# Denominators as extra columns of the numerator matmuls, in a linear-attention and mixture-of-experts kernel

## The chip, the core and the metric

The kernel runs on one core of one Trainium2 chip. Its metric is the device time of one execution in microseconds (us). The engines are PE (matmuls, with PEld for its weight loads), DVE (elementwise work), ACT (activations and copies), POOL and SP (which here mostly issue transfers).

## The reference

```python
# per batch b and head h: seq 576, head_dim 64 (8 batches, 8 heads)
q_p, k_p = phi(q), phi(k)                  # phi(x) = x + 1 for x > 0, exp(x) otherwise
kv  = einsum('bhsd,bhse->bhde', k_p, v)
z   = sum(k_p, axis=2)
num = einsum('bhsd,bhde->bhse', q_p, kv)
den = einsum('bhsd,bhd->bhs', q_p, z)[..., None] + 1e-06
x   = (num / den), as 4608 rows of 512
P   = exp(x @ w_gate - max), then 8 times: P /= P.sum(1) + 1e-9; P /= P.sum(0) + 1e-9; P *= N / E
out = sum over 8 experts e of P[:, e] * (relu(x @ w1[e]) @ w2[e])
```

## The kernel before

**Stages.** The front computes the attention in 16 blocks, one for each batch and half of its heads (four heads), and with it expert 0 of the second part on the token groups that are complete. After it come the routing probabilities P (a Sinkhorn loop of eight rounds) beside the rest of expert 0, and from about 172 us experts 1 to 7, in nine units of 512 tokens each, with a seven-product scheme in place of eight block products in both layers (`block7` for the first, `unit` for the second).

**Order.** Nothing is scheduled by hand. Each step is a task of a small planner (`_Plan`), with an engine or a choice of engines, an assumed duration, dependencies, and the buffers it takes and uses; `ranks`, a long string of numbers, gives priorities (and in places the engine) to the tasks of the front. The planner runs through the tasks and emits each step's instructions at its turn, so its order is the program order on each engine. An engine works through its own instructions in that order. The semaphore waits between engines are put in by the layer below, which follows, tile by tile, who reads and writes what; it knows nothing of the planner's buffers.

**One attention block.** k, q and v are loaded (L274, tiles kqin and vin). ACT takes exp (L290), DVE makes `min(max(x + 1, 1), exp x)` into `t` (L303, L306), and v is copied to `vv` beside a column of ones (L234 on ACT, L236 on DVE; these two lines are also all other copies). PE multiplies k^T by v in 18 matmuls (L335) into `kv_ps`, two PSUM banks; the ones give z, the sum of k, as column 65 of each head. That product is masked and moved to `kvz` (L346 on ACT, L348 on DVE). PE transposes q in two pieces of five and four (L363, `qt_ps`) and they are copied to `qpT`. The division then goes like this:

- `f_den` (L378): ten matmuls with the z columns as the moving operand, two columns each, into `den_ps`;
- `f_rd` (L384, L386): DVE adds 1e-6 to the 20 denominators of a row and takes their reciprocals (`rden`);
- `f_num` (L402): ten matmuls of 128 columns into `num_ps`, in three pieces of 4, 4 and 2, each in a PSUM bank of its own;
- `f_xn` (L407): DVE multiplies each piece by the reciprocals into `xn`;
- `f_xt` (L418): PE transposes `xn` in two groups of five, and ACT or DVE copies each (L234, L236) into `xT`.

**PSUM.** Besides the kv pair there is the pool `aps` with two buffers of one bank under the tag "att". In the front `qt_ps`, `den_ps`, `num_ps`, `xt_ps` and the routing logits (`lg_ps`, L437, read by ACT at L441) take turns in it, each as a new tile; later the column sums of the Sinkhorn loop (`cs_ps`, L476), the product R of each pair of `block7` (PE writes at L737 and L742, ACT reads at L771, DVE at L780 as `h<-att`), and one tile of the last unit. The planner's own counterpart is `p_att`, a pool of two. In the first block two of the numerator pieces are in the banks `ye0` and `ye1`.

**Expert work.** `hq` (L590) is the first layer of expert 0, four matmuls of 512 columns to a task, and `ye` (L859) its second; PE fills the front with them. `yw` (L510) are warm-up matmuls on zeros in the first 20 us.

Of the kernel before, what the change touches and what calls it, by code (L numbers as in the profile page):

```python
# [122 lines left out]
def kernel(  # L123
# [35 lines left out]
    aps = ctx.enter_context(tc.tile_pool(name="aps", bufs=2, space=PSUM))  # L159
# [33 lines left out]
    p_vv, p_kvz, p_qpT, p_xn, p_rden = (S_.pool(2) for _ in range(5))  # L193
    p_att, p_hq, p_h = S_.pool(2), S_.pool(2), S_.pool(2)
    p_xst, p_s2, p_s5 = (S_.pool(2) for _ in range(3))
# [48 lines left out]
    v_land, kv_id = [], []  # L244
# [6 lines left out]
    def att(b, g):  # L251
        n = 2 * b + g
        pr = n - 100.0

        def ps_home(i):
            if n < 1 and i < 2:
                return p_ye[i], yps, f"ye{i}"
            return p_att, aps, "att"
# [80 lines left out]
        tkv = fadd(("pe", 0.54), f_kv, deps=[tph["k"]] + tvv, acq=[gkv], use=[gvv, gt["k"]], prio=pr)  # L339
# [17 lines left out]
        for j0, j1 in ((0, 5), (5, NJ)):  # L357
            gp = S_.grp(p_att)

            def f_qt(_, j0=j0, j1=j1, gp=gp):  # L360
                gp["tile"] = aps.tile([P, 5, 2, PW], FP16, tag="att", name="qt_ps")
                for j in range(j0, j1):
                    nc.tensor.transpose(gp["tile"][:, j - j0, :, :].rearrange("p h w -> p (h w)"),  # L363
                                        gt["q"]["tile"][:, j, 2:4, :].rearrange("p r d -> p (r d)"), ident)
# [7 lines left out]
        gden, grd, gxn = S_.grp(p_att), S_.grp(p_rden), S_.grp(p_xn)  # L372

        def f_den(_):
            gden["tile"] = aps.tile([P, 5, 2, 2], FP32, tag="att", name="den_ps")
            for i, j in enumerate(js):
                for hh in range(2):
                    nc.tensor.matmul(gden["tile"][:, i, :, hh],  # L378
                                     lhsT=gq["tile"][:, hh, j:j + 2, :].rearrange("p j w -> p (j w)"),
                                     rhs=gz["tile"][:, hh, :, D], start=True, stop=True)  # L380

        def f_rd(_):
            grd["tile"] = fp.tile([P, 5, 4], FP32, tag="rden", name="rden")
            nc.vector.tensor_scalar(out=grd["tile"], in0=gden["tile"].rearrange("p i r h -> p i (r h)"),  # L384
                                    scalar1=1e-6, scalar2=None, op0=ALU.add)
            nc.vector.reciprocal(grd["tile"], grd["tile"])  # L386
        tden = fadd(("pe", 0.26), f_den, deps=tq + tz, acq=[gden], use=[gq, gz], prio=pr)
        trd = fadd(("dve", 0.5), f_rd, deps=[tden], acq=[grd], use=[gden], prio=pr)

        def f_xa(_):  # L390
            gxn["tile"] = fp.tile([P, 5, 4, D], FP16, tag="xn", name="xn")
        txa = fadd(("none", 0.0), f_xa, deps=[tden], acq=[gxn], prio=pr)
        txn = []
        for i0, i1 in ((0, 2), (2, 4), (4, 5)):
            hn = ps_home(i0 // 2)
            gn = S_.grp(hn[0])

            def f_num(_, i0=i0, i1=i1, gn=gn, hn=hn):
                gn["tile"] = hn[1].tile([P, 2, 2, 2, D], FP32, tag=hn[2], name="num_ps")
                for i in range(i0, i1):  # L400
                    for hh in range(2):
                        nc.tensor.matmul(gn["tile"][:, i - i0, :, hh, :],  # L402
                                         lhsT=gq["tile"][:, hh, js[i]:js[i] + 2, :].rearrange("p j w -> p (j w)"),
                                         rhs=gz["tile"][:, hh, :, 0:D], start=True, stop=True)

            def f_xn(_, i0=i0, i1=i1, gn=gn):
                nc.vector.tensor_tensor(  # L407
                    out=gxn["tile"][:, i0:i1], in0=gn["tile"][:, 0:i1 - i0].rearrange("p i r h e -> p i (r h) e"),
                    in1=grd["tile"][:, i0:i1, :, None].broadcast_to([P, i1 - i0, 4, D]), op=ALU.mult)
            t1 = fadd(("pe", 0.12 * (i1 - i0)), f_num, deps=[tden, txa], acq=[gn], use=[gq, gz], prio=pr)  # L410
            txn.append(fadd(("dve", 0.14 + 0.275 * (i1 - i0)), f_xn, deps=[t1, trd, txa], use=[gn, grd, gxn], prio=pr))
        for c2 in range(2):
            gx = S_.grp(p_att)

            def f_xt(_, c2=c2, gx=gx):
                gx["tile"] = aps.tile([P, S], FP16, tag="att", name="xt_ps")
                for i in range(5):
                    nc.tensor.transpose(gx["tile"][:, 64 * js[i]:64 * js[i] + P],  # L418
                                        gxn["tile"][:, i, 2 * c2:2 * c2 + 2, :].rearrange("p r e -> p (r e)"), ident)
# [10 lines left out]
    def logits(b2):  # L430
        gl = S_.grp(p_att)

        def f_l(_):
            gl["tile"] = aps.tile([P, NJ, E], FP32, tag="att", name="lg_ps")
# [12 lines left out]
    def sinkhorn():  # L447
# [10 lines left out]
        for it in range(8):  # L458
# [15 lines left out]
            def f_c(_, gc=gc):  # L474
                gc["tile"] = aps.tile([P, E], FP32, tag="att", name="cs_ps")
# [20 lines left out]
    gate = const.tile([P, 4], FP32, tag="gate", name="gate")  # L496
    warm = const.tile([P, 512], FP16, tag="warm", name="warm")
# [175 lines left out]
    def block7(e, g, gW, tW):  # L673
# [49 lines left out]
        def pair(gi):  # L723
            gX, gR, gZ, gs2, gs5 = (S_.grp(p) for p in (p_hq, p_att, p_ye[3], *((p_e2, p_e5) if e == 0 else (p_s2, p_s5))))
            kx = {id(gX): (hqp, "hq"), id(gR): (aps, "att")}
# [3 lines left out]
            def pm(lhs, b, w, g_, first, deps, pr):  # L729
                def f_m(_):  # L730
                    if first:
                        pl, tag = kx[id(g_)]
                        g_["tile"] = pl.tile([P, 2, 256], FP32, tag=tag, name=tag)
# [89 lines left out]
    def unit_plain(e, g, gW=None, tW=None):  # L823
# [5 lines left out]
        if e > 0:  # L829
            zp[1], zp[2], zp[3] = (p_ye[0], yps, "ye0"), (p_hq, hqp, "hq"), (p_att, aps, "att")  # L830
# [22 lines left out]
        for tt in range(1 if e > 0 else 0, 4):  # L853
            for half in range(2):
                def f_y(_, half=half, tt=tt):
                    if half == 0:
                        gy[tt]["tile"] = zp[tt][1].tile([P, 512], FP32, tag=zp[tt][2], name=zp[tt][2])
# [237 lines left out]
    for d, k_ in zip(chain, chain[1:]):  # L1095
# [3 lines left out]
        0:-50.0024 36:8.7509 38:8.7566 40:-50.0207 42:-49.9982 43:8.7608 44:-50.0228 45:8.7578 46:-50.0192 47:-50.0138  # L1099
        49:8.7452:act 50:-49.9982 51:-50.0108 52:-50.0204:act 54:8.7572 55:-50.0216 56:8.7563 57:-49.9985:act  # L1100
        58:-50.0222 59:-50.0213 61:-50.0117 62:-50.0036 63:-50.012 64:8.759 65:-50.0135 66:-98.0291 67:-50.012
        68:8.7602:dve 69:-49.9994 70:-50.0129:act 71:-50.015 73:-50.0144 75:-49.9886 77:-50.0129 78:-49.9988
        79:-50.0186 80:8.7587 81:-50.0207 82:-50.0027 84:-50.0198 85:-49.9829 86:-49.9985:act 88:-98.021
        89:-50.015:act 90:-50.0201 91:8.7617:dve 92:-50.0195 93:-50.0219 95:-50.0162 96:8.7575 97:-50.0201 98:-50.0186
        99:8.7464 100:-98.0051 101:-50.0195 102:-50.0144:act 103:-50.0141 104:-50.0198 106:8.7632 108:8.7575
        110:-49.9844 112:-50.0216 114:-50.0006 116:8.7575 117:-50.0132 118:-50.0006 119:-50.021 120:-50.0192
        121:-49.9982 123:-50.0201:dve 124:-50.0159 125:-50.0225:dve 127:-50.0138 128:-50.0105:dve 129:8.762
        130:-50.0213 131:-98.0054 132:-50.0189 134:-49.9787 135:-50.0207 136:-49.9859 137:-50.003 138:-50.0018
        139:-50.0228 140:-50.0153 141:-50.0093:dve 142:-49.9811 143:-50.0003:dve 144:-50.0156 146:-50.012 148:-50.0147
        150:-50.0237 151:-50.021 152:8.7593 153:-50.0204 154:-50.0192 155:-50.0156 157:-50.0003:act 158:-50.0159  # L1110
        159:8.7368:dve 161:-50.0117 162:-50.0147:act 163:-50.0021 164:-50.0213 165:-50.0222 166:8.7443 168:-50.021
        169:-50.0231 170:-50.0168 171:-50.0267 172:-50.0216 173:-50.0144 174:-50.0228 175:-50.0228:dve 176:-50.0201
        177:-49.9787:act 179:-50.0063 181:-50.006 183:-50.0144 184:-50.0189 185:-50.0189 187:-50.0168 189:-50.0048
        191:8.7584 192:-49.9802 193:-50.0225 194:-50.0255 195:-50.0201 196:-50.0219 198:-50.0195 199:-50.0132
        200:-50.0207:dve 202:-50.0249 203:-50.0144 204:-50.0015 205:-50.0213:dve 206:-98.0237 207:-50.012 209:-50.0183
        210:-50.0204 211:-50.0258 212:-50.0288 213:-50.0189 214:-50.0237 215:-49.9808 216:-49.9856:act 217:-50.0219
        218:-50.0117:dve 219:8.7602 221:-50.0153 223:-49.9991 225:-50.0015 226:-50.0165 227:-50.0225 228:-50.0162
        229:-98.0078 230:-50.0165 232:-50.0087:dve 233:-98.0054 234:8.7512:dve 236:-50.0216 237:-98.0051:act
        238:-50.0246 239:-50.0165:dve 240:-50.0219 241:-98.0048 243:-50.027 244:-50.0195 245:-50.0135 246:-50.0126
        247:-50.0228 248:-50.0123 249:-50.0159 250:-50.018:act 251:-98.0228 252:-49.9826 253:-50.018 255:-50.0213  # L1120
        257:-50.018 259:-50.0162 260:-50.0231 261:-98.0063 262:-50.0282 263:-50.012 264:-50.0003 266:-50.0117:dve
        267:-50.0159 268:8.7464:act 270:-50.0195 271:8.7509:act 272:-98.0054 273:-50.0168 274:-50.0162 275:-98.0246
# [125 lines left out]
```

## Time and profile before

| | |
|---|---|
| median of 3 runs (960.19 to 960.27) | 960.21 us |
| the profiled execution, and its span | 960.04 us, 958.3 us |
| PE, DVE, ACT busy | 950.7, 768.7, 571.7 us |
| `den_ps` matmuls in all (L378) | 160, median 166 ns |
| `num_ps` matmuls in all (L402) | 160, median 220 ns |
| DVE for one block's division: L384, L386, L407 | 0.173, 0.278, 2 x 0.684 and 0.419 us |

The profile gives each instruction's start and length on its engine, what ended the idle time before it, and a chain of waits followed back from the last instruction. PE's matmuls are pipelined: a matmul of 512 columns is shown with 379 ns, and the next starts 216 ns after it. What a matmul takes from PE is the step to the next start.

### The profile page before, as it was taken

The numbers are of one execution on the slowest core, as the hardware profiler recorded it, in microseconds if no ns is written. First come the engines' busy times: TensorE is split into PE (matmuls) and PEld (weight loads), VectorE is DVE, ScalarE is ACT, GpSimd is POOL, SyncE is SP. The second block draws the span as 40 slices with busy tenths as digits, with TensorE's granted clock in tenths as the row PEclk, the third lists the DMA queues.
The fourth block names the chain that finished last, engine by engine and source line by source line (L and its number), as shares of the span: only waits on it lengthen the run. The fifth ranks groups of instructions, "written<-read, shape, count | busy, mean of one in ns | idle before, by whom it ended". The sixth has DMA issues, their size and how long they took to land.

```text
span 958.3 us, 18782 instructions
## 1 busy us (share of the span) xinstructions
PE 950.7 (99%) x7265; PEld 650.3 (68%) x7265; DVE 768.7 (80%) x1529; ACT 571.7 (60%) x1032; POOL 153.4 (16%) x199
## 2 busy tenths in 40 slices
PE   9999999999999999999999999999999999999998
PEld 4656666566676667766676666766677666766676
DVE  6988888878887787888877788877878788877776
ACT  6897855765555555555555555555555555555552
POOL 4100000111112211221112211221112211111111
PEclk9999999999999999999999999999999999999999
DMA  9985983344145421544125431644215441425545
GB/s 316 346 313 207 289 261 101 44 100 100 55 133 116 106 81 49 126 110 100 56 89 111 108 94 46 150 103 109 64 61 112 110 99 56 138 78 153 155 106 133
DMA packets 109946, 121.83 MB, mean 127 GB/s; under 512 B 7840, under 2 KB 92960, under 8 KB 109856
## 3 DMA queue, kind: packets, MB, share of 16 engines
q1 hardware_dynamic: 84320, 96.23, 32.1%
q0 software_dynamic: 25136, 23.87, 14.6%
q8 instruction: 57, 0.93, 0.4%
q10 hardware_dynamic: 400, 0.52, 0.2%
q14 instruction: 33, 0.27, 0.1%
HBM read 119.69 MB, written 17.69 MB: 143 GB/s over the span
## 4 chain that ended last, share of the span: by engine, by line
PE 95%; DMA 2%; ACT 1%; DVE 1%; issue 0%; POOL 0%; SPq 0%; DVEq 0%; ACTq 0%
PE ye L997 34%; PE hq L737 20%; PE att L737 10%; PE ye L859 7%; PE Zye L997 6%; PE Zye L737 5%; PE hq L742 4%; PE hq L590 2%; DMA kqin<-in_k_dram 2%; PE att L742 2%; PE Zye L742 1%; PE xt_ps L418 1%; PE kv_ps L335 1%; PE num_ps L402 1%; PE qt_ps L363 1%; ACT e L290 1%
## 5 line engine op out<-in xcount | busy, mean ns | idle before, releaser
L1011 DVE SCALAR_TENSOR_TENSOR acc<-ye,P_sb,acc 128x256 f32<-128x256 f32 x620 | 266.4, 476 | 105.8 <-PE ye L997 104.0
L997 PEld LDWEIGHTS <-S 128*128 128x128 f16 x1984 | 194.1, 98 | 45.9 <-issue 0.2
L1021 POOL TENSOR_TENSOR acc<-acc,h 128x256 f32<-128x256 f32 x124 | 102.9, 847 | 601.1 <-ACT h L1018 601.1
L997 PE MATMUL ye<-h,S 128*128 128x256 f16 x1488 | 192.8, 273 | 0.0
L997 PEld LDWEIGHTS <-h 128*128 128x128 f16 x1488 | 145.6, 98 | 39.9
L777 ACT ACTIVATE h<-hq 128x512 f16<-128x512 f32 x134 | 80.1, 597 | 142.0 <-PE hq L737 124.0
L737 PEld LDWEIGHTS <-W 128*128 128x128 f16 x896 | 87.7, 98 | 81.1
L737 PE MATMUL att<-xs,W 128*128 128x512 f16 x448 | 133.2, 379 | 0.0
L737 PE MATMUL hq<-xs,W 128*128 128x512 f16 x448 | 133.2, 379 | 0.0
L737 PE MATMUL hq<-xs,w 128*128 128x512 f16 x448 | 124.1, 379 | 0.0
L780 DVE CUSTOM_DVE_ANT_0 h<-att,s 128x512 f16<-128x512 f32 x126 | 86.4, 686 | 23.5 <-ACT s L764 23.0
L737 PEld LDWEIGHTS <-w 128*128 128x128 f16 x672 | 65.8, 98 | 54.5
L774 ACT ACTIVATE h<-Zye 128x512 f16<-128x512 f32 x134 | 80.1, 598 | 35.2 <-PE Zye L737 28.0
L1018 ACT ACTIVATE h<-Zye,P_sb 128x256 f32<-128x256 f32 x124 | 52.1, 471 | 78.1 <-PE Zye L997 78.1
L764 ACT COPY s<-hq 128x512 f32<-128x512 f32 x126 | 73.5, 583 | 35.4 <-PE hq L737 31.3
L780 DVE CUSTOM_DVE_ANT_0 h<-hq,s 128x512 f16<-128x512 f32 x126 | 86.3, 685 | 9.0 <-PE hq L737 9.0
L757 ACT COPY Zye<-hq 128x512 f32<-128x512 f32 x134 | 77.9, 581 | 20.2 <-PE hq L737 17.0
L968 DVE TENSOR_TENSOR S<-h 128x1024 f16<-128x1024 f16 x124 | 84.7, 683 | 5.8 <-ACT h L777 5.8
L771 ACT COPY s<-att 128x512 f32<-128x512 f32 x126 | 74.5, 591 | 0.0
L859 PE MATMUL ye<-w,h 128*128 128x512 f16 x296 | 73.8, 379 | 0.0
L737 PE MATMUL Zye<-xs,w 128*128 128x512 f16 x224 | 66.6, 379 | 0.0
L997 PE MATMUL Zye<-w,h 128*128 128x256 f16 x496 | 64.3, 273 | 0.0
(119 smaller groups left out, 1096.1 us busy)
## 6 DMA issues: line engine op xcount, KB each, us to landing
xs<-xd SPq DMA_DIRECT2D x196, 256.0 KB, 4.1
w<-in_moe_w_dram POOLq DMA_DIRECT2D x48, 256.0 KB, 4.2
out_dram<-acc SPq DMA_DIRECT2D x67, 128.0 KB, 2.4
kqin<-in_k_dram SPq DMA_DIRECT2D x12, 576.0 KB, 5.6
kqin<-in_q_dram SPq DMA_DIRECT2D x12, 576.0 KB, 6.8
vin<-in_v_dram SPq DMA_DIRECT2D x12, 576.0 KB, 7.7
xs<-xd SPq DMA_DIRECT2D x49, 128.0 KB, 2.5
xd<-xT SPq DMA_DIRECT2D x27, 128.0 KB, 6.2
```

The lines of the kernel that those rows point to most:

```text
L737: nc.tensor.matmul(dst, lhsT=lhs(0, c), rhs=X(b)(c), start=(first and c == 0), stop=(c == 1), skip_group_check=True)
L757: nc.scalar.copy(out=Zt[1], in_=gX["tile"])
L764: nc.scalar.copy(out=gs2["tile"], in_=gX["tile"])
L771: nc.scalar.copy(out=gs5["tile"], in_=gR["tile"])
L774: nc.scalar.activation(out=hd(0, 0), in_=Zt[1], func=AF.Relu)
L777: nc.scalar.activation(out=hd(1, 0), in_=gX["tile"], func=AF.Relu)
L780: nc.vector._custom_dve(TENSOR_ADD_SAT, out=dst, in0=ps, in1=sb, s0=3.0e38, s1=0.0)
L859: nc.tensor.matmul(gy[tt]["tile"], lhsT=hx(f, P * tt, P), rhs=gw2["tile"][:, f, :], start=(f == 0), stop=(f == NFT - 1))
L968: nc.vector.tensor_tensor(out=gS[i]["tile"], in0=a0, in1=a1, op=op)
L997: nc.tensor.matmul(bank(g_)[:, s, :], lhsT=lhs(s, kk), rhs=rhs(kk), start=(new and s == 0 and kk == 0), stop=(kk == 3), skip_group_check=True)
L1011: nc.vector.scalar_tensor_tensor(out=dst(), in0=bank(g_)[:, s, :], scalar=P_sb[:, gg, e:e + 1], in1=dst(), op0=ALU.mult, op1=ALU.add)
L1021: nc.gpsimd.tensor_tensor(out=dst(), in0=dst(), in1=gst["tile"], op=ALU.add)
```

## The change

The separate denominator matmuls go. Each numerator matmul takes all of a head's 65 columns of `kvz` for both row halves, 130 columns, so that every 65th output column is a denominator. The ten matmuls are in two pieces: six into the two kv banks and four into both att banks. For each piece the denominators get their 1e-6 (`f_ra`, on ACT or DVE as the planner chooses), DVE takes reciprocals and multiplies. `att2` is now one tile of both att banks, allocated once; `att_bank` gives the half whose turn it is, to every user of the old tag. Two dependencies are new: a block's kv product waits for piece A of the block two before, and piece A for that of the block before. The string `ranks` is new throughout, and with it the order of the front.

```diff
-    aps = ctx.enter_context(tc.tile_pool(name="aps", bufs=2, space=PSUM))
+    aps = ctx.enter_context(tc.tile_pool(name="aps", bufs=1, space=PSUM))
...
+    att2 = aps.tile([P, 2, 512], FP32, tag="att", name="att")
+
+    def att_bank(dt=FP32):
+        b = att2[:, (len(p_att["order"]) - 1) % 2]
+        return b if dt == FP32 else b.bitcast(dt)
...
-        tkv = fadd(("pe", 0.54), f_kv, deps=[tph["k"]] + tvv, acq=[gkv], use=[gvv, gt["k"]], prio=pr)
+        tkv = fadd(("pe", 0.54), f_kv, deps=[tph["k"], num_a[n - 2] if n > 1 else None] + tvv, acq=[gkv],
+                   use=[gvv, gt["k"]], prio=pr)
...
-                gp["tile"] = aps.tile([P, 5, 2, PW], FP16, tag="att", name="qt_ps")
+                gp["tile"] = att_bank(FP16)[:, 0:640].rearrange("p (j h w) -> p j h w", h=2, w=PW)
...
-        def f_den(_):
-            gden["tile"] = aps.tile([P, 5, 2, 2], FP32, tag="att", name="den_ps")
...
-        for i0, i1 in ((0, 2), (2, 4), (4, 5)):
-            hn = ps_home(i0 // 2)
-            gn = S_.grp(hn[0])
+        for i0, i1 in ((0, 3), (3, 5)):
+            ni = i1 - i0
+            gns = [S_.grp(p_kv)] if i0 == 0 else [S_.grp(p_att), S_.grp(p_att)]
+            grd = S_.grp(p_rden)
...
+            def f_num(_, i0=i0, i1=i1, gns=gns, grd=grd):
+                gns[0]["tile"] = kvps.tile([P, 2, 512], FP32, tag="kv", name="num_ps") if i0 == 0 else att2
+                grd["tile"] = fp.tile([P, 2, 6], FP32, tag="rden", name="rden", bufs=4)
                 for i in range(i0, i1):
                     for hh in range(2):
-                        nc.tensor.matmul(gn["tile"][:, i - i0, :, hh, :],
+                        nc.tensor.matmul(gns[0]["tile"][:, hh, 2 * D1 * (i - i0):2 * D1 * (i - i0 + 1)],
                                          lhsT=gq["tile"][:, hh, js[i]:js[i] + 2, :].rearrange("p j w -> p (j w)"),
-                                         rhs=gz["tile"][:, hh, :, 0:D], start=True, stop=True)
+                                         rhs=gz["tile"][:, hh].rearrange("p r e -> p (r e)"), start=True, stop=True)
...
+            def f_ra(eng, num=num, grd=grd, ni=ni):
+                o, i_ = grd["tile"][:, :, 0:2 * ni], num()[:, :, :, D]
+                if eng == "act":
+                    nc.scalar.activation(out=o, in_=i_, func=AF.Identity, bias=eps_t[:, 0:1])
+                else:
+                    nc.vector.tensor_scalar(out=o, in0=i_, scalar1=1e-6, scalar2=None, op0=ALU.add)
+
+            def f_rd(_, grd=grd, ni=ni):
+                nc.vector.reciprocal(grd["tile"][:, :, 0:2 * ni], grd["tile"][:, :, 0:2 * ni])
...
+            t1 = fadd(("pe", 0.12 * ni), f_num, deps=tq + tz + [txa, num_a[n - 1] if n > 0 and i0 == 0 else None], acq=gns + [grd], use=[gq, gz], prio=pr)
...
-                gx["tile"] = aps.tile([P, S], FP16, tag="att", name="xt_ps")
+                gx["tile"] = att_bank(FP16)[:, 0:S]
...
-                gc["tile"] = aps.tile([P, E], FP32, tag="att", name="cs_ps")
+                gc["tile"] = att_bank()[:, 0:E]
...
-                        pl, tag = kx[id(g_)]
-                        g_["tile"] = pl.tile([P, 2, 256], FP32, tag=tag, name=tag)
+                        g_["tile"] = (hqp.tile([P, 2, 256], FP32, tag="hq", name="hq") if g_ is gX else
+                                      att_bank().rearrange("p (a b) -> p a b", a=2))
```

## The prediction

> **What bounds the kernel now.** I read the page first, then busy time by stage, then the chain of waits and the order of time on PE and DVE.
>
> ```profile
> span 958.3 us, 18782 instructions
> PE 950.7 (99%) x7265; PEld 650.3 (68%) x7265; DVE 768.7 (80%) x1529; ACT 571.7 (60%) x1032; POOL 153.4 (16%) x199
> 20.00:131.00 111.00, 109.16 (x1256) 68.29 (x1255) 95.03 (x197) 89.18 (x137) 7.32 (x10) 1.00 0.90 283
> 131.00:172.00 41.00, 40.67 (x296) 28.47 (x294) 36.10 (x86) 23.50 (x44) 0.00 (x0) 1.00 0.49 159
> 172.00:958.00 786.00, 782.24 (x5555) 543.36 (x5553) 625.47 (x1216) 447.83 (x838) 137.44 (x172) 1.00 0.40 99
> ```
>
> The columns of the last three rows are the stretch, its length, then busy us of PE, PEld, DVE, ACT and POOL, the granted clock, the DMA share and GB/s. PE is busy in every stage at a granted clock of 1.00, so a microsecond of PE work or of PE waiting after 20 us is a microsecond of the run. In the front (20 to 131 us) DVE and ACT are also 86% and 80% busy. The profiled execution took 960.04 us (span 958.3), 0.17 below the median of 960.21.
>
> ```profile
> L402 PE MATMUL num_ps<-kvz,qpT 128*128 128x128 f16 x140 | 13.6, 220 | 1.2 <-DVE xn L407 1.2
> L378 PE MATMUL den_ps<-kvz,qpT 128*128 128x2 f16 x140 | 5.7, 166 | 0.0
> 12.26 0.41 PE L378 MATMUL den_ps<-kvz,qpT 128*128 128x2 f16 x10
> 12.52 0.38 PE L510 MATMUL yw<-warm 128*128 128x512 f16 x1
> ```
>
> 140 of the 160 denominator matmuls lie after 20 us. Their mean of 166 ns is a pipelined length; what they take from PE is the step to the next start, 12.52 - 12.26 = 0.26 us for ten, 27 ns each by the median of all such steps.
>
> ```profile
> 86.42 0.90 PE lg_ps L437 x36
> 87.32 0.02 issue
> 87.34 0.24 ACT P_sb L441
> 87.58 0.04 issue
> 87.62 0.44 PE xt_ps L418 x5
> ```
>
> This piece of the chain prices a hand-over: PE has given its last matmul at 87.16, ACT starts 0.18 later, and PE starts 0.04 after ACT ends. PE lost 0.46 us here, since nothing stood between the write and the next write of that bank.
>
> **Removed: the denominators.** 140 x 27 ns = 3.8 us of PE, all on the path (the first two blocks' 20 matmuls lie where warm-up matmuls fill PE anyway). The numerators get 130 columns for 128: 140 x 2 columns at 0.42 ns (216 ns for 512) is 0.1. Net **-3.7**.
>
> DVE keeps its load: 0.17 + 0.28 + 2 x 0.68 + 0.42 = 2.24 us per block before. Afterwards 0.95 (0.684 for 512 elements and 0.419 for 256 give 0.265 per 256) + 0.68, reciprocals of 12 and 8 elements at 0.23 and 0.20 (0.278 at 20, 0.203 at 8), and one add of 0.17, 2.23 us. The other add goes to ACT (half of the 32 adds do in the built order), 16 x about 0.25 (nearest row: L441, 0.262), 4 us of an engine that idles 22 us in the front. Cost on the path 0, up to 2 if that cover fails.
>
> **Added: waits.** The old pool gave each use of a bank its own tile. Now att2 is one tile of two banks, and the built program's waits (no time is in them) show that every access to it follows every earlier one on another engine, whichever bank it touches. A DVE copy of bank 1 waits for ACT's copy of bank 0, and PE's write of either bank waits for both. Before 131 us 43 reads on ACT or DVE wait for the other's read; in the old program the two copies of a block carry no such wait.
>
> Front. At nine of PE's waits after 20 us the chain from its own last write is longer than the PE work that stands between. Seven are two copies in turn against four 512-column matmuls (0.86 us):
>
> ```profile
> L236 DVE COPY xT<-xt_ps x16: 444/450/458, 20.4 to 128.9; 128x576 f16<-128x576 f16 x16
> L234 ACT COPY xT<-xt_ps x14: 620/639/702, 20.9 to 128.6; 128x576 f16<-128x576 f16 x14
> ```
>
> 0.18 + 0.64 + 0.04 + 0.45 + 0.04 - 0.86 = 0.49 twice; with the qpT copies (ACT 0.59 and 0.70, DVE 0.42 and 0.49) in place of one or both, 0.44, 0.44, 0.46, 0.58 and 0.44. One pair has somewhat more cover (0.15), and one xt follows a logits group at once and waits for a whole qpT copy (0.71). Sum 4.2; the 0.46 at 87.6 us goes with the old order, so **+3.7**. The bounds are 0 (ACT and DVE never meet) and 8 (each of the 36 cross-reads after the second block adds another 0.1 behind other work on in-order queues); I take the sum, because the same arithmetic gives the 0.46 that the trace has.
>
> Start. Piece A of block 0 sits in the two kv banks and piece B in both att banks, so kv and qt of block 1 wait for block 0's xn. Before, they run at 14.77 and 14.18, beside it. By rows: ACT ends block 1's second exp at 13.5 (13.16 before; its first copy now waits for both transposes), DVE its min at 14.3, two reciprocals to 14.7, xn 0.95 to 15.65 and 0.68 to 16.3; qt 16.4 to 17.0; its copies in turn (0.70, 0.42) to 18.3; ten numerators to 18.9; add, reciprocal and xn of 0.68 to 19.8; block 0's xt to 20.4; its copies in turn to 21.75; block 1's xt 21.8 to 22.4, against 19.21 to 19.77 before. At 24.3 us PE had done 20 hq matmuls; now 8 by 24.1. 12 x 0.216 - 0.2 = **+2.4** (0 if the front's other stalls absorb it, 3 if not and a step slips).
>
> 131 to 172 us: a column-sum matmul of the Sinkhorn loop waits for a DVE read of the other bank (0.69 + 0.22 less 0.44 of work, 0.47), one product for ACT and then DVE (0.66), a third 0.24: **+1.4** (0 to 3).
>
> Expert stage. The last 1147 DVE instructions and 1311 PE groups stand in the same order in both programs, but each pair's first write of an att bank now waits for the preceding pair's read of the other one. So the trace of before prices it.
>
> ```profile
> 501.67 0.59 PE L737 MATMUL hq<-xs,w 128*128 128x512 f16 x2
> 501.74 0.67 DVE L780 CUSTOM_DVE_ANT_0 h<-att,s 128x512 f16<-128x512 f32 x1
> 502.10 0.59 PE L737 MATMUL att<-xs,W 128*128 128x512 f16 x2
> ```
>
> The DVE row ends at 502.42 and PE writes at 502.10: 0.32 too early for the new wait. I went through all such neighbours after 172 us. 13 of them overlap, by 0.41 once, 0.32 five times, 0.12 six times and 0.05 once, twice per expert where DVE also makes the weight combinations. 2.8 + 13 x 0.04 = **+3.3**. Low end 2 (a first stall relieves the second), high end 5 (some twenty more clear the wait by only 0.1).
>
> The Trainium skill, "Perfetto Trace Analysis", section "Matmuls", wants independent matmul groups to rotate through different PSUM banks, so that ACT's and DVE's emptying of one overlaps the next group. It speaks against this change; the 0.46 at 87.6 us, where the wanted bank was still being read, agrees. By that rule the time is that of the sum below; were the rotation kept, it would be 956.5.
>
> **Sum.** -3.7 + 3.7 + 2.4 + 1.4 + 3.3 = +7.1 on 960.04, 967.1; at the median 967.3. The other stalls of the front (1.3 at 71 us behind a kqin load, 0.9 in small ones) I leave as they are; that adds 2 to either side.
>
> **Rivals.**
> The saving alone, 956.5 (chance 0.06). The waits are real but cost nothing, because PE has other work in its queue and reads end early; that decides as soon as the waits and the start together cost less than 1.8 us of the 10.8 I count (3.7 - 1.9). For it: the same arithmetic finds only two of the old program's stalls, so it may miss covers too, and the order was planned with two banks. Against it: that order interleaves only four matmuls at seven places, and the 13 overlaps are in the trace. The Trainium skill, "PSUM — Partial Sum Buffer", section "Specifications (TRN2)", says ScalarE and VectorE read PSUM in parallel at full rate where they meet in no bank; the trace agrees (ACT's qpT copy from 9.94 for 0.59, DVE's from 10.21 for 0.49), but a wait stands before it.
>
> About no change, 960 to 962 (0.10). The start's 2.4 is absorbed by the stalls at 24 to 30 and at 71 us, and half of the front's 3.7 is too: 967.3 - 2.4 - 1.9 - 2 = 961.
>
> Much slower, 973 (0.20). DVE and ACT become the bound between 20 and 110 us. There they were already 94% and 93% busy from 40 to 70 us. If the 36 cross-reads each hold an in-order engine for half of a copy (0.29), that is 10 us of their idle 38; from the point where more than half of it falls in 20 to 70 us, PE waits for them: +5 to +6.
>
> The change does not do what it says (0.01). The built program has 320 fewer PE rows, which are the denominators and their weights.
>
> **Numbers.** The forecast has 0.63. Slower by over 0.2% (0.2% is 1.9 us, about what a measurement can tell from no change) is the forecast and the much slower case, with a sliver of the no-change case: 0.84. Within it 0.09, faster 0.07. The range takes the unknowns of the sum down to 962 and the larger part of the much slower case, up to 973.
>
> **What would show it.** Right: no den rows; 140 numerators after the start at about 60 ns steps; hq starting in earnest near 22.4; PE idle before att writes released by ACT or DVE copies; in the expert stage PE waiting for `h<-att` about 13 times, 0.1 to 0.45 each. Wrong: xT copies of two banks side by side; block 1's xt before 21; no PE waits after 172 us; or a front in which DVE has no idle time at all.

## The result, and the profile after

The changed kernel took **970.62 us** (median of 5 runs, 970.22 to 971.7) against 960.21 before: a ratio of 1.0111 (95% interval 1.0097 to 1.0126), 10.4 us slower. The forecast was 967.3 with a range of 962 to 973. The profiled execution took 971.33 us (span 969.5), 0.7 above the median; the span of before was 958.3, so the two traces differ by 11.2.

The page of the changed kernel:

```profile
span 969.5 us, 18505 instructions
...
PE 952.2 (98%) x7105; PEld 644.8 (67%) x7105; DVE 769.5 (79%) x1529; ACT 576.9 (59%) x1049; POOL 153.2 (16%) x199
```

Its busy time by stage (stretch, its length, then busy us of PE, PEld, DVE, ACT and POOL, the granted clock, DMA share, GB/s):

```profile
20.00:131.00 111.00, 105.45 (x1079) 62.61 (x1079) 93.55 (x195) 90.15 (x146) 6.10 (x9) 1.00 0.90 281
131.00:172.00 41.00, 39.32 (x317) 27.12 (x315) 35.92 (x88) 23.36 (x43) 0.00 (x0) 1.00 0.47 148
172.00:969.00 797.00, 790.57 (x5594) 546.79 (x5592) 629.37 (x1220) 452.43 (x845) 137.76 (x172) 1.00 0.40 98
```

The 160 denominator rows are gone (7265 to 7105), the clock is 1.00 throughout, and DVE has the same load. PE now stands idle for 5.55, 1.68 and 6.43 us in the three stages (length less busy time), where before it was 1.84, 0.33 and 3.76.

What PE waits for, from the list of its waits after 20 us (us in total, times, longest):

```profile
PE att L423 <- DVE xT L241: 2.6, 5, 1.2
PE att L743 <- DVE h L786: 2.3, 8, 0.5
PE att L423 <- ACT qpT L239: 0.8, 2, 0.4
PE att L423 <- DVE qpT L241: 0.6, 1, 0.6
PE att L423 <- ACT xT L239: 0.5, 2, 0.3
...
PE att L364 <- DVE xT L241: 0.4, 1, 0.4
...
PE att L442 <- ACT xT L239: 0.3, 1, 0.3
```

(L423 is the xn transpose, L364 the q transpose, L239 and L241 the copies on ACT and DVE, L743 and L786 the old L737 and L780.) Each is a write of an att bank that waits for a copy or a read. The list shows idle time only up to the modelled end of the matmul before, so it is short by up to 0.16 us at each place (379 - 216 ns). For sums I add, over all pairs of successive PE starts, what the step is longer than the usual step, the median for that line and shape in the same run (the excess). In us, by time:

| | steps at their usual length | excess 0–33 | 33–134 | 134–175 | 175–end | excess in all |
|---|---|---|---|---|---|---|
| before | 942.68 | 4.4 | 4.7 | 0.4 | 0.4 | 9.95 |
| changed | 938.64 | 7.7 | 9.1 | 2.4 | 5.9 | 25.18 |
| the experiment after_banks | 938.50 | 6.2 | 3.3 | 0.3 | 0.8 | 10.67 |

938.64 - 942.68 + 25.18 - 9.95 = +11.2, the difference of the spans. The saving is there; the waits ate it nearly four times over.

One place in full, the timeline of the changed kernel from 97.75 us (start, length, engine, line, what, and in brackets the idle time before it and what ended that):

```profile
97.75 0.38 PE L364 MATMUL att<-ident,t 128*128 128x128 f16 x4
...
97.97 0.44 PE L423 MATMUL att<-ident,xn 128*128 128x128 f16 x5
...
98.25 1.03 PE L597 MATMUL hq<-xT,w 128*128 128x512 f16 x4
98.45 0.42 DVE L241 COPY qpT<-att 128x512 f16<-128x512 f16 x1 [0.75 <-PE att L423]
...
98.91 0.64 ACT L239 COPY xT<-att 128x576 f16<-128x576 f16 x1 [0.19 <-DVE qpT L241]
...
99.59 0.72 PE L423 MATMUL att<-ident,xn 128*128 128x128 f16 x10 [0.32 <-ACT xT L239]
```

PE fills one bank (97.75) and the other (97.97). DVE's copy of the first bank begins only when the second bank is written too; ACT's copy of the second bank begins 0.04 after DVE's of the first ended; PE's next write follows 0.04 after ACT. Four `hq` matmuls of 0.86 stand between: 0.18 + 0.42 + 0.04 + 0.64 + 0.04 - 0.86 is 0.46, and the step is 0.485 too long.

### The profile page after: what moved, and what is told of

The parts are those of the page before. It is cut to its first block, busy times and chain, and to the rows that moved or that the text cites. A ratio compares the mean times of both kernels' runs of the same rounds, so it can differ in the third digit from the quotient of the medians.

```text
span 969.5 us, 18505 instructions
## 1 busy us (share of the span) xinstructions
PE 952.2 (98%) x7105; PEld 644.8 (67%) x7105; DVE 769.5 (79%) x1529; ACT 576.9 (59%) x1049; POOL 153.2 (16%) x199
## 4 chain that ended last, share of the span: by engine, by line
PE 89%; DVE 8%; ACT 2%; issue 1%; DVEq 0%; ACTq 0%
PE ye L1004 33%; PE hq L743 19%; PE att L743 10%; PE Zye L1004 5%; PE Zye L743 5%; PE ye L866 4%; PE hq L597 3%; PE hq L748 2%; DVE h L786 1%; DVE acc L1018 1%; PE att L423 1%; PE att L748 1%; PE yw L517 1%; PE att L364 1%; DVE S L975 1%
## 5 line engine op out<-in xcount | busy, mean ns | idle before, releaser
L743 PEld LDWEIGHTS <-W 128*128 128x128 f16 x896 | 87.6, 98 | 86.0 <-issue 6.6
L743 PE MATMUL att<-xs,W 128*128 128x512 f16 x448 | 133.3, 379 | 2.3 <-DVE h L786 2.3
L743 PE MATMUL hq<-xs,W 128*128 128x512 f16 x448 | 133.3, 379 | 0.0
L743 PE MATMUL hq<-xs,w 128*128 128x512 f16 x448 | 124.1, 379 | 0.0
L786 DVE CUSTOM_DVE_ANT_0 h<-att,s 128x512 f16<-128x512 f32 x126 | 86.6, 687 | 26.1 <-ACT s L770 25.2
L743 PEld LDWEIGHTS <-w 128*128 128x128 f16 x672 | 65.7, 98 | 54.9 <-issue 0.3
L780 ACT ACTIVATE h<-Zye 128x512 f16<-128x512 f32 x134 | 80.1, 598 | 36.6 <-PE Zye L743 27.2
L786 DVE CUSTOM_DVE_ANT_0 h<-hq,s 128x512 f16<-128x512 f32 x126 | 86.5, 686 | 9.1 <-PE hq L743 9.0
L743 PE MATMUL Zye<-xs,w 128*128 128x512 f16 x224 | 66.7, 379 | 0.0
L1004 PE MATMUL ye<-w,h 128*128 128x256 f16 x496 | 64.3, 273 | 0.0
```

The lines of the kernel that those rows point to most:

```text
L743: nc.tensor.matmul(dst, lhsT=lhs(0, c), rhs=X(b)(c), start=(first and c == 0), stop=(c == 1), skip_group_check=True)
L780: nc.scalar.activation(out=hd(0, 0), in_=Zt[1], func=AF.Relu)
L786: nc.vector._custom_dve(TENSOR_ADD_SAT, out=dst, in0=ps, in1=sb, s0=3.0e38, s1=0.0)
L1004: nc.tensor.matmul(bank(g_)[:, s, :], lhsT=lhs(s, kk), rhs=rhs(kk), start=(new and s == 0 and kk == 0), stop=(kk == 3), skip_group_check=True)
```

## The experiments

My theory was the forecast's: the two banks are one tile, so every access waits for every earlier one of another engine, whichever bank it touches. The rivals: the new order of the front (and the new dependencies through the kv banks) costs the time; DVE or ACT had become the bound; the start is what is lost. Except where said, each experiment keeps the order of instructions on every engine as in the kernel it is made from, so that only waits differ. In after_late, before_share and before_share_late not one instruction is added or moved; in after_banks and banks_share_late, where piece B is two tiles, DVE gets 24 more and ACT 8.

**after_banks: a tile for each use.**

```diff
-    aps = ... tile_pool(name="aps", bufs=1, space=PSUM)
+    aps = ... tile_pool(name="aps", bufs=2, space=PSUM)
...
-    att2 = aps.tile([P, 2, 512], FP32, tag="att", name="att")
     def att_bank(dt=FP32):
-        b = att2[:, (len(p_att["order"]) - 1) % 2]
-        return b if dt == FP32 else b.bitcast(dt)
+        return aps.tile([P, 512 if dt == FP32 else 1024], dt, tag="att", name="att")
...  # piece B: two tiles, so its add and its multiply become one instruction per bank
+                    gns[0]["tile"] = [att_bank(), att_bank()]
```

> The changed kernel in its own order, but each use of an att bank has a tile of its own; piece B is two tiles, so its add and its multiply are two instructions each (DVE: 0.15 to 0.32 us more per block). Whole-tile waits: the waits of experts 1 to 7 (4 to 5), those at 131 to 175 us (2) and most of the front's 4 go, the start's 3 stay: 970.6 - 10 = 960.5 (959 to 963). Rival 'the new order' (order and the new dependencies through the kv banks cost it): 968 to 971. Rival 'DVE is the bound in the front': 3.5 us more of DVE work there make 971 to 974.

Measured: 956.86 (956.45 to 957.21), ratio to before 0.9963 (0.9949 to 0.9976). The whole loss goes, and this version is faster than both kernels. More goes than I had expected (959 to 963): by the table, 1.5 us of the start's loss, which I had let stay, and 5.8 in the front, where I had put most of 4. The same steps as above, in its timeline:

```profile
93.44 0.39 PE L362 MATMUL att<-ident,t 128*128 128x128 f16 x4
...
93.66 0.44 PE L432 MATMUL att<-ident,xn 128*128 128x128 f16 x5
93.86 0.42 DVE L239 COPY qpT<-att 128x512 f16<-128x512 f16 x1 [0.26 <-PE att L362]
...
93.94 1.03 PE L606 MATMUL hq<-xT,w 128*128 128x512 f16 x4
...
94.36 0.64 ACT L237 COPY xT<-att 128x576 f16<-128x576 f16 x1
...
94.80 0.72 PE L432 MATMUL att<-ident,xn 128*128 128x128 f16 x10
```

DVE starts after its own bank's transposes, although PE is still writing the other one, and PE goes on behind the four `hq` without a wait. The order of the front and the dependencies through the kv banks are the same as in the changed kernel, so they are not what cost it. Nor is DVE's own work the bound: between 20 and 134 us it now does more in the same time, and PE is busier. The stage in the changed kernel:

```profile
20.00:134.00 114.00, 108.09 (x1102) 64.25 (x1102) 95.21 (x198) 91.35 (x149) 6.10 (x9) 1.00 0.88 274
```

and in after_banks:

```profile
20.00:134.00 114.00, 112.76 (x1182) 69.86 (x1183) 102.75 (x234) 97.48 (x167) 6.36 (x10) 1.00 0.93 290
```

**after_late and banks_share_late: sharing in one part only.** In after_late the pool with att2 belongs to the front, and a pool of two single banks is opened when the front's pools close, at about 134 us; banks_share_late is the converse.

```diff
+    aps = front.enter_context(tc.tile_pool(name="aps", bufs=1, space=PSUM))
...
     def att_bank(dt=FP32):
+        if late:
+            return late[0].tile([P, 512 if dt == FP32 else 1024], dt, tag="att", name="att")
...
     def f_close(_):
         front.close()
+        late.append(ctx.enter_context(tc.tile_pool(name="aps2", bufs=2, space=PSUM)))
```

> The changed kernel in its own order; att2 is shared in the front only, and from the closing of the front's pools on (about 134 us) each use has a tile of its own. Whole-tile waits: 970.6 less 4 to 5.5 in the expert stage and 1.5 to 2.5 before it: 963 to 965, with no PE wait on a read of h<-att after 175 us. Rival 'the new order': 970 to 971.

> The converse of after_late: the changed kernel in its own order, each use of an att bank with a tile of its own in the front, and one tile for both banks from the closing of the front's pools on. If the waits of the two parts add up: 956.9 + (970.6 - 964.8) = 962.7, and PE waits on reads of h<-att again. If a late front hides or makes them: under 960 or over 965.

Measured: 964.81 (963.71 to 964.98; ratio 1.0043, 1.0031 to 1.0056) and 963.30 (962.8 to 964.19; ratio 1.0030, 1.0018 to 1.0042). Against after_banks' 956.86, sharing costs 7.95 us in the front alone, 6.4 after it alone, and 13.8 in both: the parts nearly add up (14.4). In after_late no wait on `h<-att` is left after 175 us; in banks_share_late they are back (PE's waits after 131 us):

```profile
PE att L758 <- DVE h L801: 1.9, 8, 0.4
PE att L494 <- ACT Zye L778: 1.0, 1, 1.0
PE att L763 <- DVE h L801: 0.5, 1, 0.5
PE att L494 <- DVE h L801: 0.4, 1, 0.4
```

**before_share and before_share_late: the old kernel with one tile.** The same `att2` and `att_bank` put into the kernel before, with its denominators and its order, in all stages or only after the front.

> The kernel before, every instruction in its old order on every engine; only the two att banks are one tile. Whole-tile waits (the forecast's theory): 18 places of the front where the chain from PE's last write is longer than the PE work between, 7 us by the copies' durations, 13 waits of 3.7 us in experts 1 to 7, 1 to 2 between: 960.2 + 10 to 14 = 970 to 974. Rival 'the new order': the waits are hidden and the new order of the changed kernel is what costs: 960 to 962.

> The kernel before in its old order; only from the closing of the front's pools on are the two att banks one tile. The forecast's working for the expert stage and the stretch before it, 3.3 + 1.4: 960.2 + 4.7 = 965; by the waits that the changed kernel shows there, 5.8: 966. If the waits belong to the new order: 960 to 961.

Measured: 988.79 (988.13 to 989.06), ratio 1.0295 (1.0281 to 1.0309), far above the 970 to 974 that I had expected, and 966.18 (965.3 to 967.44), ratio 1.0059 (1.0047 to 1.0072), as expected. After the front, sharing costs the old program 5.8 us, much as it costs the new one. In the front it costs it 22.6 more (988.8 - 966.2), where I had worked out 7 from the same local arithmetic (the top of PE's waits in before_share):

```profile
PE att L408 <- DVE xn L413: 3.3, 9, 0.6
PE att L368 <- DVE xn L413: 2.4, 7, 0.5
PE att L383 <- ACT xT L239: 2.0, 3, 0.9
PE att L383 <- DVE xn L413: 1.7, 2, 1.1
```

Numerators (L408), q transposes (L368) and denominators (L383) wait for an xn multiply, 18 times in these rows; in the kernel before, with the same instructions, one of PE's waits between 20 and 131 us is for an xn, and in the changed kernel one after 20 us. I had counted the lengths of the copies and multiplies alone; what their engine still has to do before it reaches them was left out, and that seems to be the difference here. It was not measured by itself.

**after_start and banks_start: block 0 divided as before.** Its ten denominators and three pieces return, two of these in `ye0` and `ye1`, so that block 1 need not wait for its xn. Here the planner made the order anew behind the start, in the whole front; both kernels have the same order and differ only in the tiles.

```diff
+        if n < 1:
+            ...  # f_den, f_rd, three pieces of f_num and f_xn as in the kernel before
-        for i0, i1 in ((0, 3), (3, 5)):
+        for i0, i1 in ((0, 3), (3, 5)) if n > 0 else ():
```

> The changed kernel, but block 0 alone divides as before (ten denominator matmuls, three numerator pieces, two of them in ye0 and ye1), so that block 1's kv and qt do not wait for its xn. If the start's delay counts in full: block 1's xt near 19.5 instead of 21.9 us and 970.6 - 2.6 = 968. If later stalls absorb it: xt early, but 970 to 971.

> The order of after_start on every engine, but each use of an att bank has a tile of its own (as in after_banks). If after_start's 988.75 comes of whole-tile waits that the planner does not know, they go here and the start's gain shows: 956.9 less 1 to 2 = 955 to 956. If block 0's division, or the order that the planner makes around it, is what cost it: 970 or more.

Measured: 988.75 (987.16 to 990.81; ratio 1.0297, 1.0279 to 1.0315) and 972.94 (971.76 to 974.32; ratio 1.0135, 1.0119 to 1.0150). For after_start both cases that I had foreseen failed; for banks_start the second came (970 or more). The shared tile costs 15.8 us in this order too, but the order costs 16.1 by itself over after_banks. So these two say nothing of the start, and I wrote the order out.

**after_fixed and banks_fixed: the same start, the order behind it held.** The planner's run is replaced by a list: the first two blocks as in after_start, everything after them as in the changed kernel.

```diff
-    S_.run()
...  # seq: the list of tasks, in order
+    for w in seq.split():
+        n, *en = w.split(":")
+        t = S_.t[int(n)]
+        for g in t["acq"]:
+            g["pool"]["order"].append(g)
+        t["fn"](en[0] if en else "none")
```

> The changed kernel with its own order written out as a list, so that nothing after the start is moved; block 0 divides as before (as in after_start), and the first two blocks stand in after_start's order. If the start's delay counts in full: 970.6 - 2.6 = 968.0. If the later waits absorb it: 970 to 971. If after_start's 18 us came of block 0's division itself and not of the order behind it: 985 or more.

> The same list with a tile of its own for each use of an att bank. From after_banks (956.86): if the start's delay counts, 956.9 - 1 to 2 = 955 to 956; if it is absorbed, 957. If the order that the planner made behind the start is what cost banks_start 16 us over after_banks, nothing of these 16 is left here.

Measured: 970.80 (970.52 to 972.1; ratio 1.0112, 1.0096 to 1.0127) and 956.73 (955.96 to 958.1; ratio 0.9968, 0.9956 to 0.9981): neither differs from the kernel that it is made from by more than the runs scatter. Block 0's division costs nothing that these runs can show, and the order behind it cost the 16 us. The start is earlier by less than I had hoped (block 1's xt at 21.27 us in after_fixed, where I had wanted 19.5), and what it gains is mostly lost again. The timeline of PE shows where. In the changed kernel:

```profile
21.90 0.72 PE L423 MATMUL att<-ident,xn 128*128 128x128 f16 x10 [1.22 <-DVE xT L241]
...
25.58 0.69 PE L335 MATMUL kv_ps<-vv,t 64*128 64x130 f16 x18
...
32.28 0.69 PE L335 MATMUL kv_ps<-vv,t 64*128 64x130 f16 x18
```

and in after_fixed:

```profile
21.27 0.72 PE L462 MATMUL att<-ident,xn 128*128 128x128 f16 x10 [0.23 <-DVE xn L447]
...
25.08 0.69 PE L335 MATMUL kv_ps<-vv,t 64*128 64x130 f16 x18 [0.41 <-DVE vv L241]
...
32.14 0.69 PE L335 MATMUL kv_ps<-vv,t 64*128 64x130 f16 x18
```

Block 1's transposes come 0.63 earlier, with two `hq` matmuls ahead of them besides; block 2's kv product then waits for DVE's copy `vv`, and block 3's comes 0.14 earlier than it did. In banks_fixed the same PE instruction, counted from the end, comes 1.9 us earlier than in after_banks at 24 us and 0.5 earlier at 31 us.

**banks_ye: piece A of block 0 in `ye0` and `ye1`**, the order of after_banks unchanged.

> The order of after_banks unchanged; only piece A of block 0 is in the banks ye0 and ye1, two tiles, in place of the kv banks, so that block 1's kv product does not wait for block 0's multiply (0.86 us of PE idle at 14.5 us in after_banks). If that wait counts: 956.9 - 0.9 = 956.0. If block 1's qt and its xt, which still follow block 0's xn on DVE, set the start: 956.9, no change.

Measured: 956.83 (955.91 to 957.85), ratio 0.9967 (0.9955 to 0.9980). The kv product of block 1 starts at 14.06 instead of 15.55 and `hq` at 20.02 instead of 21.29, so PE is 1.3 us ahead there; at 31 us 0.3 of it is left, and in the time of the kernel nothing is gained that the runs can show.

## Why the prediction was right, and where it was off

**The mechanism and the sign** were right: after_banks shows that the shared tile, and nothing else in the change, makes it slower. With own tiles the time is 956.86, where I had put 956.5 for a kept rotation. That this is so near is in part luck: against before, after_banks has 1.8 us more excess up to 33 us and 1.4 less from there to 134, since the new order is without the old stalls of 1.3 and 0.46 us. What the rule of the Trainium skill that I weighed is after ("Perfetto Trace Analysis", "Matmuls": independent groups on different banks, so that the emptying of one overlaps the next group) is worth 13.8 us here (970.62 - 956.86). But the changed kernel writes two banks in turn as well; it lost the overlap to the waits on the one tile, so different banks were not enough. The range held, though one term lies outside its own bounds (the expert stage, 5.5 for 2 to 5): its upper end of 973 had been set for another case.

**Removed (-3.7).** PE's steps at their usual length fell by 4.0, the first two blocks' 0.5 among them; after_banks gains 3.35 net (960.21 - 956.86), with 0.7 more excess than before. DVE's load stayed (769.5 for 768.7), the ACT add took 0.277 and 0.269 where I had taken 0.25. Right.

**Front (+3.7).** The excess from 33 to 134 us rose by 4.4. The nine places are there, and the sizes too: seven steps of 0.47 to 0.61 too long where I had 0.44 to 0.58, 0.20 where I had 0.15, and 0.721 where I had 0.71 for the transpose behind the logits, here in the timeline:

```profile
120.54 1.05 PE L442 MATMUL att<-wg_sb,xT 128*128 128x8 f16 x36
...
121.62 0.49 DVE L241 COPY qpT<-att 128x640 f16<-128x640 f16 x1 [0.72 <-PE att L442]
...
122.17 0.44 PE L423 MATMUL att<-ident,xn 128*128 128x128 f16 x5 [0.58 <-DVE qpT L241]
```

That is 4.5 for 4.2. Four places more, 0.515 at 72.2, 0.496 at 88.2, 0.545 at 116.3 and 0.412 at 123.0 us, I had not (the last two hold 0.12 that nearly every step out of a kv product has, stall or not). There the copy that PE waits for stands behind other work of its engine, at 116.3 us behind another copy. The rise is only 4.4 because the old stalls at 71 (1.3) and 87 us (0.46) are gone; against the same order with own tiles it is 5.8.

**Start (+2.4).** Block 1's xt came at 21.90 (forecast 21.8), and the excess to 33 us rose by 3.3, 0.5 of it the denominators' room. But I had counted this delay as a cost of its own; in after_fixed, banks_ye and banks_fixed an earlier start is mostly lost again behind DVE's and ACT's work on the next blocks (such as `vv` above): 1.1, 1.3 and 1.9 us at 22 to 24 us are 0.1, 0.3 and 0.5 at 31 us. What is left is less than the runs can tell, whose intervals leave 1.2 us or so open, and none of the three takes back the whole delay. The bound of 0 that I gave it ("if the front's other stalls absorb it") was the better value as far as block 0's placement goes.

**131 to 172 us (+1.4).** 2.0. The three steps that I listed were 0.601 (the column sum), 0.691 (the product read by ACT and then DVE) and 0.175 too long for 0.47, 0.66 and 0.24. Two more, 0.513 at 138.8 and 0.506 at 172.4 us, wait for other data; in after_late, without the sharing there, the first is there too (0.513), the second is 0.278.

**Expert stage (+3.3)** is the step that was off most: 5.5. The 13 places came as read from the old trace: 0.375 to 0.381 five times (0.36 forecast), 0.171 to 0.173 six times (0.16), 0.655 (0.45) and 0.105 (0.09), 3.7 in all. One of them in the timeline:

```profile
400.56 0.59 PE L743 MATMUL hq<-xs,w 128*128 128x512 f16 x2
400.63 0.68 DVE L786 CUSTOM_DVE_ANT_0 h<-att,s 128x512 f16<-128x512 f32 x1
...
401.36 0.59 PE L743 MATMUL att<-xs,W 128*128 128x512 f16 x2 [0.21 <-DVE h L786]
```

The other 1.8 lies in six places from 178 to 217 us that I had declared free, because in the old trace these neighbours do not overlap. But the last 1147 DVE instructions, which stand in the same order in both programs, begin only at 217.5 us in the changed kernel: the DVE work of all six places comes before that, where the two orders differ. In the old trace the routing probabilities were done at 182.3 us, 9.5 after PE began with expert 1; now they are done at 181.5, 1.4 after it. So DVE multiplies rows of the output by them (L897) while the first pairs run. In three of the six places, 1.2 us in all, PE's write of an att bank waits for a read that starts late (the timeline of one):

```profile
189.93 1.27 DVE L897 TENSOR_SCALAR acc<-acc,P_sb 128x512 f32<-128x512 f32 x3
...
191.12 0.68 DVE L786 CUSTOM_DVE_ANT_0 h<-att,s 128x512 f16<-128x512 f32 x1
...
191.85 0.59 PE L743 MATMUL att<-xs,W 128*128 128x512 f16 x2 [0.33 <-DVE h L786]
```

In the other three (0.6) PE goes to a ye or hq bank; one of them, 0.17 at 206 us, is in after_late too (0.21). With own tiles the excess after 175 us is 0.8 in all (after_late). "The trace of before prices it" failed where the order on DVE and the moments are not those of the old trace. Where they are, it held: in before_share_late, the old program in its old order, the excess after 175 us rises by 3.5 (3.95 for 0.43), close to the 3.3.

**The rivals.** The much slower case, 973 by DVE and ACT as the bound: after_banks gives DVE more work and is faster than before, so their work alone is not the bound. It takes away the cross-reads as well, so it does not test whether these hold the two engines up. Against that stands the trace of the changed kernel: from 40 to 70 us, the stretch that the case names as fullest, DVE and ACT are busy for 27.1 and 27.9 of 30 us, and PE is idle for 0.41. What there is of that case is the four late copies, under 2 us; the measured 970.6 came close to 973 because the start, the front, the Sinkhorn stretch and the expert stage were each somewhat larger. No change: an earlier start is mostly absorbed, as that case had it, but the front's waits were not.

## What to carry to other kernels

What this dependency layer follows is the tile and not the bank: two buffers put into one tile for the sake of one instruction that spans them lose their independence everywhere they are used, here 13.8 us for a gain of 3.4. Make the buffers two tiles and split the one instruction that spans them, even where that costs the next engine some work. And price a new wait with the queue that its releaser stands in, at the moment at which the new program gets there; the old trace shows lengths well and moments only where nothing before them has moved.

## What was not expected of the hardware

In the two kernels with the unlucky order the granted TensorE clock fell to half for some us. Busy time of banks_start in three stretches, columns as above (the clock is 1.00, 0.57, 1.00):

```profile
71.00:74.00 3.00, 0.90 (x14) 0.66 (x12) 3.00 (x6) 3.00 (x6) 0.00 (x0) 1.00 0.00 0
74.00:78.00 4.00, 4.00 (x16) 1.56 (x14) 2.83 (x8) 1.73 (x6) 0.00 (x0) 0.57 0.00 0
78.00:82.00 4.00, 4.00 (x27) 2.13 (x26) 2.92 (x10) 1.21 (x4) 0.00 (x0) 1.00 0.45 140
```

PE had been busy for 0.90 of 3 us, with one idle stretch of 1.9; then matmuls of 512 columns took steps of 427 ns instead of 216 for some 3.5 us. This cost banks_start about 2.9 us of its 16 (1.7 here, 1.2 near 144 us), so that waits which come close together cost more here than their own length. In after_start the clock was at 0.50 for longer, from 144 to 157 us with PE busy for 8.4 of the 13; so part of the 15.8 us between these two kernels is the clock, and how much was not measured. The Trainium skill, "TensorE: Matmul & The Clock Gate", Part 1, says that the clock is halved after an idle window of about 3.4 us and full again after a busy one of that length. The 3.5 us of the slow stretch at 74 us agree, but the window before it was not wholly idle. In the changed kernel, none of whose steps after 22 us is more than 0.72 too long, the clock stayed at 1.00.
